# Block-sparse attention with an MLP behind it: diagonal mask by affine_select, built-in gelu, casting loads, and the second MLP product next to the next batch's attention

## The chip, the cores and the metric

One core of one Trainium2 chip. The metric is device time in microseconds (us) of one execution. Most numbers inside an execution come from one profiled execution of each kernel, which is called "the trace". Times below are medians of 4 executions for a changed kernel and of 4 to 7 for the kernel before, on the same chip. With one core an execution is called slow when it is over 1.5% above the fastest one of the same kernel.

## The reference

Four batches, eight heads, 768 tokens, head size 64. Per head, keys are averaged over blocks of 64 tokens; each query keeps its own block and the three blocks with the best gate score, and of those only what is causal. The result (3072 tokens of 512 features) goes through a two-layer MLP with the tanh form of gelu.

```python
k_rep = k.reshape(B, H, n_blocks, block, D).mean(axis=3)
gate_scores = np.einsum('bhsd,bhnd->bhsn', q, k_rep)
... # blocks after the query's own: -1e9; top 3 and the own block are kept
scores = scale * np.matmul(q, k.transpose(0, 1, 3, 2))
mask = mask & (pos[:, None] >= pos[None, :])
... # softmax over what is kept, times v, heads put side by side: x
h = x @ w_in                                   # 512 -> 2048
g = 0.5 * h * (1.0 + np.tanh(c * (h + 0.044715 * h * h * h)))
return g @ w_out                               # 2048 -> 512
```

## The kernel before

It works on pairs of heads, 16 pairs in all, four to a batch. For each pair it transposes q and k on TensorE, makes the block sums of k and the gate scores in fp32, turns the choice of blocks into 12 extra rows of q and k (so that one matmul gives scores with the block mask), adds the causal triangle by one more matmul for each diagonal block, applies Exp, and multiplies by v (this product is called PV below). A column of ones in v gives the softmax's denominator.

The MLP of a finished batch is cut into 30 pieces per batch (S1, the first product with gelu; S2, the second product), and one piece is emitted between the stages of the next batch's attention. In batch 0 there are no pieces yet, and matmuls on zeros that nothing reads stand in.

```python
def emit_moe(n):
    for _ in range(n):
        if moe_q:
            moe_q.pop(0)()
        elif warm[0] > 0:                      # batch 0: fillers
            ...
                nc.tensor.matmul(wt[:, 0:128], ident16, zsrc, start=True, stop=True)
...
# weights: fp32 loads, then one cast each on ScalarE
nc.sync.dma_start(out=win32, in_=moe_w_in.rearrange("(ci p) f -> p ci f", p=128))
nc.sync.dma_start(out=wout32, in_=moe_w_out.rearrange("(fi p) c -> p fi c", p=128))
nc.scalar.copy(out=w_in16, in_=win32)
nc.scalar.copy(out=w_out16, in_=wout32)
...
# block sums of k: fp32 matmuls against a two-column indicator
for c in range(NC):
    nc.tensor.matmul(mt[:, 456 + 2 * c:458 + 2 * c],
                     k_sd[:, c].rearrange("p h d -> p (h d)"), blockind,
                     start=True, stop=True)
...
# scores of one group of two key chunks, then the triangle, then Exp
    nc.tensor.matmul(st[:, cb:cb + 128], ident16, tri16, start=False, stop=True)
nc.scalar.activation(out=at[:, 0:wa + wb], in_=st[:, 0:wa + wb],
                     func=AF.Exp, bias=0.0, scale=SCALE)
...
# S1: 256 tokens x 256 features at a time; gelu in four operations
nc.scalar.square(out=hsq, in_=hflat)
nc.vector.scalar_tensor_tensor(out=uu, in0=hsq, scalar=CC, in1=hflat, op0=ALU.add, op1=ALU.mult)
nc.scalar.activation(out=th, in_=uu, func=AF.Tanh, bias=0.0, scale=C2)
nc.vector.scalar_tensor_tensor(out=..., in0=th, scalar=1.0, in1=hflat, op0=ALU.add, op1=ALU.mult)
```

The softmax here doesn't subtract the row's maximum and nothing guards it: scores larger than these inputs give would overflow.

## Time and profile before

| | |
|---|---|
| time | 401.99 us median of 3 before the prediction (398.93 to 406.75); 404.37 us of 4 with the run beside the changed kernel |
| TensorE busy | 372.6 us, 93% of the span |
| weight casts on ScalarE | 2 x 7.02 us |
| composed gelu, per 512 columns | 596 + 681 + 629 + about 684 ns |
| clock granted to TensorE | mean 0.95; half from 61.5 to 102.5 us but for two windows |

The page's first two parts, before: busy us with the share of the span, then two rows of 40 slices of the span, in which a digit is the busy share in tenths (9 is 90% or more), and PEclk is the granted TensorE clock in tenths.

```profile
PE 372.6 (93%) x3344; PEld 274.3 (68%) x3344; DVE 248.8 (62%) x676; ACT 265.2 (66%) x395; POOL 6.3 (2%) x30
...
PE   5999986899989999999898999999988999999996
...
PEclk9999996555999999999999989999999999999999
```

And the chain of work that ended last, by engine:

```profile
PE 69%; ACT 14%; DVE 12%; issue 2%; DMA 1%; SPq 0%; ACTq 0%
```

TensorE is at work almost all the time; of the recorded clock only slices 6 to 9, some 60 to 100 us, are low. (The profile holds the clock from its first record on, at 20.5 us in before; the 9s ahead of it are no measurement. There the fp32 transposes of q and k follow each other at 213 ns, and later, at full clock, at 109 ns: TensorE ran at half clock until then, and the mean clocks quoted are too high by that.) The windows view of before gives the busy time of each engine in a stretch (start:end, length, then each engine's busy us with its number of instructions, the granted clock, the DMA share, GB/s):

```profile
core 0: us, PE busy (x) PEld busy (x) DVE busy (x) ACT busy (x) POOL busy (x), PEclk, DMA share, GB/s
102.50:152.70 50.20, 47.37 (x452) 34.28 (x449) 36.49 (x94) 36.71 (x58) 0.00 (x0) 1.00 0.30 66
152.70:234.20 81.50, 77.33 (x736) 55.86 (x736) 52.68 (x157) 55.42 (x87) 0.00 (x0) 1.00 0.23 59
234.20:310.00 75.80, 72.68 (x697) 53.55 (x697) 53.45 (x154) 53.40 (x84) 0.00 (x0) 0.98 0.04 15
310.00:402.00 92.00, 85.77 (x611) 54.28 (x609) 57.17 (x95) 59.69 (x108) 0.00 (x0) 1.00 0.10 35
```

In each stretch TensorE is 93 to 96% busy at or near full clock, so after the first hundred microseconds it is TensorE's work that sets the time. What went wrong before that shows in the ScalarE timeline of before (start, length, engine, line, operation, out<-in, then in brackets the idle time ahead of it and what ended it):

```profile
54.32 7.02 ACT L167 CAST w_in_138<-win_180 128x8192 f16<-128x8192 f32 x1
61.23 0.93 ACT L292 ACTIVATE at_1_2_963<-st_1_2_962 128x896 f16<-128x896 f32 x1
...
63.92 7.02 ACT L168 CAST w_out_139<-wout_181 128x8192 f16<-128x8192 f32 x1
...
73.41 0.92 ACT L292 ACTIVATE at_0_0_1114<-st_0_0_1113 128x896 f16<-128x896 f32 x1
```

Two casts of 7 us stand among the Exps. The last Exp of a pair (61.23) waits behind the first cast, the first Exp of the next pair (73.41) behind the second, and the next pair therefore comes 24.2 us after the one before in place of 12.3.

### The profile page before, as it was taken

The numbers are of one execution on the slowest core, as the hardware profiler recorded it, in microseconds if no ns is written. First come the engines' busy times: TensorE is split into PE (matmuls) and PEld (weight loads), VectorE is DVE, ScalarE is ACT, GpSimd is POOL, SyncE is SP. The second block draws the span as 40 slices with busy tenths as digits, with TensorE's granted clock in tenths as the row PEclk, the third lists the DMA queues.
The fourth block names the chain that finished last, engine by engine and source line by source line (L and its number), as shares of the span: only waits on it lengthen the run. The fifth ranks groups of instructions, "written<-read, shape, count | busy, mean of one in ns | idle before, by whom it ended". The sixth has DMA issues, their size and how long they took to land.

```text
span 401.9 us, 8201 instructions
## 1 busy us (share of the span) xinstructions
PE 372.6 (93%) x3344; PEld 274.3 (68%) x3344; DVE 248.8 (62%) x676; ACT 265.2 (66%) x395; POOL 6.3 (2%) x30
## 2 busy tenths in 40 slices
PE   5999986899989999999898999999988999999996
PEld 4988865587855876675776677667576675675672
DVE  2556633346672894686688279568657546955963
ACT  2166698636674893884787579388568755865782
POOL 6000000000000000000000000000000000000000
PEclk9999996555999999999999989999999999999999
DMA  9999999923003914052400100000000010011011
GB/s 184 219 323 392 305 203 211 182 46 76 0 2 108 181 41 106 27 119 68 104 2 2 54 1 2 28 28 0 29 29 0 2 54 26 28 52 55 0 55 52
DMA packets 81350, 34.08 MB, mean 85 GB/s; under 512 B 75681, under 2 KB 75681, under 8 KB 80801
## 3 DMA queue, kind: packets, MB, share of 16 engines
q1 hardware_dynamic: 81312, 33.56, 34.5%
q8 instruction: 26, 0.43, 0.5%
q14 instruction: 12, 0.09, 0.1%
HBM read 27.26 MB, written 6.29 MB: 83 GB/s over the span
## 4 chain that ended last, share of the span: by engine, by line
PE 69%; ACT 14%; DVE 12%; issue 2%; DMA 1%; SPq 0%; ACTq 0%
PE hps L340 12%; DVE uu L350 4%; ACT hsq L348 3%; ACT w_in_138 L167 2%; ACT th L355 1%; DMA k_sd_65<-in_k_dram 1%; PE ops_0_4091 L367 1%; PE ops_0_2666 L367 1%; PE ops_0_5090 L367 1%; PE ops_0_4922 L367 1%; PE ops_0_5426 L367 1%; PE ops_0_5258 L367 1%; PE ops_0_4754 L367 1%; PE ops_0_4563 L367 1%; PE ops_0_1702 L367 1%
## 5 line engine op out<-in xcount | busy, mean ns | idle before, releaser
L350 DVE SCALAR_TENSOR_TENSOR uu<-hsq,hps 128x512 f16<-128x512 f16 x96 | 65.4, 681 | 51.8 <-ACT hsq L348 50.6
L340 PEld LDWEIGHTS <-w_in_138 128*128 128x128 f16 x768 | 71.9, 100 | 22.0 <-ACT w_in_138 L167 3.1
L355 ACT ACTIVATE th<-uu 128x512 f16<-128x512 f16 x96 | 60.2, 629 | 14.2 <-DVE uu L350 14.2
L348 ACT ACTIVATE hsq<-hps 128x512 f16<-128x512 f32 x96 | 56.7, 596 | 18.0 <-PE hps L340 17.7
L340 PE MATMUL hps<-xT_134,w_in_138 128*128 128x256 f16 x192 | 53.6, 279 | 6.9 <-ACT w_in_138 L167 2.9
L340 PE MATMUL hps<-xT_136,w_in_138 128*128 128x256 f16 x192 | 53.4, 279 | 0.6 <-DVE xT_136 L324 0.6
L340 PE MATMUL hps<-xT_135,w_in_138 128*128 128x256 f16 x192 | 53.6, 279 | 0.0
L340 PE MATMUL hps<-xT_137,w_in_138 128*128 128x256 f16 x192 | 53.4, 278 | 0.0
L288 PEld LDWEIGHTS <-ident_105 128*128 128x128 f16 x192 | 20.0, 104 | 10.1 <-issue 4.2
L315 DVE TENSOR_TENSOR xns<-xnr,zrec 128x384 f16<-128x384 f16 x32 | 17.7, 554 | 4.4 <-ACT xnr L313 4.3
L321 PEld LDWEIGHTS <-xns 128*64 128x64 f16 x192 | 12.0, 113 | 10.8 <-DVE xns L315 9.8
L152 PEld LDWEIGHTS <-ident_105 128*128 128x128 f16 x208 | 15.2, 112 | 0.5
L282 PEld LDWEIGHTS <-kT_0_1_145 76*128 76x128 f16 x64 | 6.7, 113 | 2.8 <-issue 1.4
L282 PEld LDWEIGHTS <-kT_0_0_144 76*128 76x128 f16 x64 | 6.6, 111 | 2.1 <-issue 0.9
L282 PEld LDWEIGHTS <-kT_1_1_147 76*128 76x128 f16 x64 | 6.1, 103 | 1.9 <-issue 0.3
L356 DVE SCALAR_TENSOR_TENSOR gT_3581<-th,hps 128x512 f16<-128x512 f16 x8 | 5.5, 684 | 2.5 <-ACT th L355 2.5
L168 ACT CAST w_out_139<-wout_181 128x8192 f16<-128x8192 f32 x1 | 7.0, 7022 | 0.0
L167 ACT CAST w_in_138<-win_180 128x8192 f16<-128x8192 f32 x1 | 7.0, 7021 | 0.0
L356 DVE SCALAR_TENSOR_TENSOR gT_1272<-th,hps 128x512 f16<-128x512 f16 x8 | 5.4, 684 | 2.6 <-ACT th L355 2.5
L282 PEld LDWEIGHTS <-kT_1_0_146 76*128 76x128 f16 x64 | 5.8, 100 | 1.6
L356 DVE SCALAR_TENSOR_TENSOR gT_2431<-th,hps 128x512 f16<-128x512 f16 x8 | 5.5, 683 | 1.4 <-ACT th L355 1.3
L180 PE MATMUL wq_218<-ident_100,q_sd_64 128*128 128x128 f32 x6 | 1.5, 426 | 4.7 <-DMA q_sd_64<-in_q_dram 4.7
(1156 smaller groups left out, 929.1 us busy)
## 6 DMA issues: line engine op xcount, KB each, us to landing
out_dram<-osb SPq DMA_DIRECT2D x24, 256.0 KB, 2.0
win_180<-in_moe_w_in_dram SPq DMA_DIRECT2D x1, 4096.0 KB, 13.9
wout_181<-in_moe_w_out_dram SPq DMA_DIRECT2D x1, 4096.0 KB, 24.2
q_sd_64<-in_q_dram SPq DMA_DIRECT2D x2, 192.0 KB, 3.0
k_sd_65<-in_k_dram SPq DMA_DIRECT2D x2, 192.0 KB, 3.7
v_sd_66<-in_v_dram SPq DMA_DIRECT2D x2, 192.0 KB, 4.2
q_sd_73<-in_q_dram SPq DMA_DIRECT2D x2, 192.0 KB, 4.5
k_sd_74<-in_k_dram SPq DMA_DIRECT2D x2, 192.0 KB, 4.6
```

The source lines that it names most:

```text
L152: nc.tensor.matmul(wt[:, 0:128], ident16, zsrc, start=True, stop=True)
L167: nc.scalar.copy(out=w_in16, in_=win32)
L282: nc.tensor.matmul(st[:, u0:u1], kt[0:76, s0:s0 + 128], qt[0:76, s0 + (u0 - cb):s0 + (u1 - cb)], start=True, stop=(bank != tri_bank),)
L288: nc.tensor.matmul(st[:, cb:cb + 128], ident16, tri16, start=False, stop=True,)
L315: nc.vector.tensor_tensor(out=xns, in0=xnr, in1=zrec.unsqueeze(2).to_broadcast([128, NC, 64]), op=ALU.mult,)
L321: nc.tensor.transpose(pvq16[0:64, qc * 128:(qc + 1) * 128], xns[:, qc, :], ident16)
L340: nc.tensor.matmul(hps[:, j, :], w_in16[:, ci, (fi + j) * 128:(fi + j + 1) * 128], xT[ci][:, t0:t0 + TCH], start=(ci == 0), stop=(ci == 3),)
L348: nc.scalar.square(out=hsq, in_=hflat)
L350: nc.vector.scalar_tensor_tensor(out=uu, in0=hsq, scalar=CC, in1=hflat, op0=ALU.add, op1=ALU.mult,)
L355: nc.scalar.activation(out=th, in_=uu, func=AF.Tanh, bias=0.0, scale=C2)
L356: nc.vector.scalar_tensor_tensor(out=gT[:, fi:fi + 2, :].rearrange("p a w -> p (a w)"), in0=th, scalar=1.0, in1=hflat, op0=ALU.add, op1=AL ...
L367: nc.tensor.matmul(ops, gT[:, fi, ti * 128:(ti + 1) * 128], w_out16[:, fi, :], start=(fi == 0), stop=(fi == NF - 1),)
```

## The change

The intent is to take work off TensorE and off the composed gelu, and to arrange the MLP anew. Diff, cut to its core:

```diff
-    nc.sync.dma_start(out=win32, ...); nc.scalar.copy(out=w_in16, in_=win32)   # and w_out
+    def load_w_in():
+        nc.gpsimd.dma_start(
+            out=w_in16, in_=moe_w_in.rearrange("(ci p) f -> p ci f", p=128))   # casts on the way
+    def load_v(p):                        # v too: fp32 in memory, fp16 in SBUF
+            nc.gpsimd.dma_start(out=v16[p % NB][:, :, hh, 0:64], in_=v[b, 2 * hp + hh]...)
...
-            nc.tensor.matmul(mt[:, 456 + 2 * c:458 + 2 * c], k_sd[:, c]..., blockind, ...)
+        nc.vector.tensor_reduce(
+            out=ks, in_=wk[:, 0:S].rearrange("p (n w) -> p n w", w=64),
+            op=ALU.add, axis=AXL.X)
...
-                nc.tensor.matmul(st[:, cb:cb + 128], ident16, tri16, start=False, stop=True)
                 ex = nc.scalar.activation(out=at[:, 0:wa + wb], ..., func=AF.Exp, ...)
+                for cb in (0, wa):
+                    nc.gpsimd.affine_select(
+                        out=at[:, cb:cb + 128], in_=at[:, cb:cb + 128],
+                        compare_op=ALU.is_ge, fill=0.0,
+                        base=0, pattern=[[1, 128]], channel_multiplier=-1)
+                # PV of one head accumulates in one PSUM bank, group by group, right after its Exp
...
-        # square, scalar_tensor_tensor, tanh, scalar_tensor_tensor; 0.5 at the end
+            g = nc.scalar.activation(out=gT[b][:, f, :], in_=hps[:, 0:S],
+                                     func=AF.Gelu_apprx_tanh, bias=0.0, scale=1.0)
...
+    for b in range(B):
+        for hp in range(HP):
+            p = b * HP + hp
+            load(p + 4)
+            if p == 2:
+                load_w_out()
+            pre(p + 2)                    # transposes, gate, mask of the pair after next
+            heads(p)
+        if b > 0:
+            s2(b - 1)                     # fills gaps of this batch's attention
+        s1(b)                             # all 16 blocks in a row: one table switch
+    s2(B - 1)
```

Normalisation now handles both heads of a pair at once (six output transposes in place of twelve), the gate is not computed for the first 128 queries (they keep all their causal blocks anyway), and the fillers of batch 0 are gone. The scheduler that lays out the instructions puts S2's matmuls, which stand behind the pairs in the program text of a batch, into gaps that it foresees in attention.

## The prediction

> **What bounds the kernel now.** TensorE, in three stages. The page gives it 93% busy, and 69% of the chain that ended last. Windows view: from 153 to 234 us four head pairs and their share of the MoE pass, 81.5 us, TensorE busy 77.3, clock 1.00; from 310 to 402 us only MoE is left, 14.4 us per 256 tokens (chain of waits: 326.1, 340.5, 354.9). Between: ScalarE's two weight casts, 7.02 us each, from 54 to 68 us stop TensorE, its clock falls to 0.5 and stays there most of the time until 102 us (0.62 and 0.59 in the windows 60:80 and 80:100).
>
> **Removed from TensorE**, by spacings in the timeline at full clock: block sums by matmul 1.29 us per pair (to a VectorE reduction), triangle matmuls 12 x 57 ns = 0.7, half the output transposes 0.36. A pair falls from about 8.5 to 6.0 us, some 40 us over 16 pairs, and 208 filler matmuls (12 us) go. Both MoE products keep their work: 1.33 us per 128 rows of d_ff and batch, 21.3 per batch; second product 16 x 222 ns = 3.6 per 128 tokens, 21.3 per batch.
> **Removed elsewhere:** per 512 columns Square 596, Tanh 629 and two VectorE operations of 681 ns become one Gelu of about 0.85 us per 768 (estimate from Exp, 0.92 for 896). The casts go.
> **Added:** 12 affine_selects per pair on GpSimd, 0.30 us each (setup ones in the trace), between Exp and PV; GpSimd-issued cast DMAs for v and the weights (the Trainium skill, "DMA: Bandwidth & Descriptors", SWDGE vs HWDGE vs iDMA: casting DMAs are GpSimd's alone; no run shows their issue time yet, I guess 1 to 3 us per v DMA); seven table loads more, 1.28 us.
>
> **Critical path after.** S1 (21.3 us per batch) and the last S2 (21.3 + 3) stay TensorE-bound. Attention becomes bound by a chain, not by an engine: two PSUM tiles serve q, k and scores alike. Instruction order shows per pair: six Exps with scores held behind PV, which waits for the selects, 5.6 us; then select, PV of head 0, issue of a v DMA (which waits for that PV and stands before head 1's select), select, PV of head 1, reciprocal, k copy (0.95), normalisation, transposes, next scores: 7 to 8 us. So about 13.4 us per pair, against 11.3 us of TensorE with S2. The first selects also queue behind eight v DMAs and both weight DMAs: first pair done at 38, not 30.
> Sum: 38 + three pairs at a partly half clock, 16 each, + 8 + S1 22 = 116; batches 1 and 2: 3 + 53 + 22 = 78 each; batch 3 (last pairs have no preparation): 73; tail 24. About 367; I take a little off for unmodelled overlap.
>
> **Predicted: 363 us, 80% range 333 to 397.** Faster by over 2%: 0.87; within 2%: 0.08; slower: 0.05.
>
> **Signs.** TensorE busy share falls to 75-85%, ScalarE to about 45%; VectorE about 50%; GpSimd waits name PE. S1 stretches of about 21 us with TensorE over 95% busy, four of them. Clock at 0.5 in much of the first attention (before 90 us), mostly 1.0 afterwards: the Trainium skill, "TensorE: Matmul & The Clock Gate", Part 1, has windows of 3.4 us; the before windows agree with that[...]. Waits of TensorE name affine_select and VectorE's k copy or normalisation. No 7 us casts.
>
> **What would make it wrong.** A v DMA issue of 4 us or more on GpSimd: above 395. Under 1 us: near 340. Clock at half in batches 1 to 3 too: attention there 22 us per pair, over 420. A better interleaving of S2 into the chain's gaps: 335. Weight DMAs slow to land (v of pair 4 shares their semaphores): start-up plus 10 to 20.

## The result, and the profile after

The changed kernel takes 357.81 us (median of 4, 357.56 to 358.47), the kernel before 404.37 us on the same chip (median of 4, 398.93 to 408.13; by the rule of 1.5% two of these four, 406.75 and 408.13, count as slow). Ratio 0.897, 95% interval 0.889 to 0.905. Ratios in this document are the mean time of one kernel's fast runs over that of the other's of the same rounds, so not quite the ratio of the medians that are quoted.

The page after, same parts, with the DMA row (mean busy share of the core's 16 DMA engines):

```profile
PE 319.0 (90%) x2352; PEld 195.1 (55%) x2352; DVE 154.6 (43%) x456; ACT 159.8 (45%) x184; POOL 88.0 (25%) x252
...
PE   3625977988999999999999999989999999999995
...
PEclk9999967667999999999999999999999999999999
DMA  9999999583004548823004832341000000100012
...
PE 72%; ACT 9%; issue 6%; DMA 5%; POOL 3%; DVE 3%; SPq 2%; ACTq 0%; POOLq 0%
```

TensorE is busy 53.6 us less (372.6 to 319.0), the span is 46.0 us shorter (401.9 to 355.9). The windows view of after: attention of batch 0, its S1 with the way to the next pair, then batch 1 from its first Exp to the table load ahead of S1, and from there to the first Exp of batch 2.

```profile
34.24:84.10 49.86, 44.60 (x339) 31.67 (x338) 28.19 (x97) 23.89 (x28) 17.74 (x52) 0.73 0.98 145
84.10:114.15 30.05, 28.63 (x183) 17.17 (x181) 7.15 (x23) 16.17 (x19) 2.23 (x4) 0.99 0.23 34
114.15:156.10 41.95, 39.34 (x377) 24.50 (x376) 28.77 (x85) 23.45 (x27) 17.67 (x52) 1.00 0.60 97
156.10:191.40 35.30, 34.62 (x217) 20.14 (x215) 8.76 (x26) 16.33 (x21) 2.23 (x4) 1.00 0.23 44
```

The first line has half clocks (0.73; about 0.64, an estimate, if the unrecorded 9.5 us up to 43.7 us are counted as half) and a DMA share of 0.98; from batch 1 on the clock is full and TensorE 94 and 98% busy. To see where the time came from, take three stretches, with the traces' times:

| stretch | before | after | difference |
|---|---|---|---|
| start to the first Exp | 22.7 | 34.2 | +11.5 |
| from there to the first Exp of pair 4, without S1 of batch 0 (20.1 us, from its first Gelu at 88.4 to 108.5 us, only in after) | 69.3 | 59.8 | -9.5 |
| the rest (12 pairs, all of the MLP; S1 of batch 0 added to after) | 309.9 | 261.8 | -48.1 |
| in the last row, TensorE busy (windows view) | 293.6 | 249.8 | -43.8 |

So almost all of the gain is TensorE work that is no longer there: 43.8 of the 48.1 us. And 11.5 us are lost at the start, which I had put down to something else. The TensorE timeline of after shows that wait:

```profile
25.46 1.30 PE L171 MATMUL wq_327<-ident_103,q_sd_242 128*128 128x128 f32 x5 [6.68 <-DMA q_sd_242<-in_q_dram]
```

TensorE stands for 6.68 us until the q of pair 2 has landed. The transposes of pair 2 stand in its order ahead of the scores of pair 0. SyncE's timeline shows when that q was issued (8.24 us, in two issues), and that the next two issues took 11.34 us; below it, the list of DMA issues of after (KB each, median us from issue to landing) shows what was under way:

```profile
8.24 1.72 SPq L68 DMA_DIRECT2D q_sd_242<-in_q_dram  x2
10.00 11.34 SPq L68 DMA_DIRECT2D k_sd_246<-in_k_dram  x2
```

```profile
w_in_181<-in_moe_w_in_dram POOLq DMA_DIRECT2D x1, 2048.0 KB, 15.7
w_out_182<-in_moe_w_out_dram POOLq DMA_DIRECT2D x1, 2048.0 KB, 33.7
...
q_sd_94<-in_q_dram SPq DMA_DIRECT2D x2, 192.0 KB, 3.7
...
q_sd_242<-in_q_dram SPq DMA_DIRECT2D x2, 192.0 KB, 11.1
```

The first q load lands after 3.7 us, that of pair 2 after 11.1 us as the median of its two issues; the later of the two landed at 25.3 us, 16.2 us after its issue. The weights now come at the same time, while the DMA row is at 9. The Trainium skill, "DMA: Bandwidth & Descriptors", section "Issuing engines are not separate DMA queues", says that loads issued by different engines run on the same 16 DMA engines and interleave. This trace agrees: SyncE's loads slow down though GpSimd issued the big ones.

Inside attention one order stands out, here at the end of a pair in batch 1 of after (a timeline of all engines, cut):

```profile
143.36 0.92 ACT L242 ACTIVATE at_1_2_1613<-st_1_2_1612 128x896 f16<-128x896 f32 x1
...
144.51 0.84 POOL L78 DMA_DIRECT2D v_161<-in_v_dram  x1 [0.62 <-PE pv_0_1536 L258]
...
145.36 0.55 POOL L252 TENSOR_SCALAR_AFFINE_SELECT at_1_2_1613<-at_1_2_1613 128x128 f16<-128x128 f16 x2
145.72 0.52 PE L258 MATMUL pv_1_1537<-v_161,at_1_2_1613 128*128 128x65 f16 x7 [0.60 <-POOL at_1_2_1613 L252]
```

The last Exp ends at 144.28, but its selects begin at 145.36, because GpSimd first waits for a PV and then issues a load of v for a later pair, 0.84 us. TensorE idles 0.60 us for it.

### The profile page after: what moved, and what is told of

It is laid out like the page before. It is cut to its first block, busy times and chain, and to the rows that moved or that the text cites. A ratio compares the mean times of both kernels' runs of the same rounds, so it can differ in the third digit from the quotient of the medians.

```text
span 355.9 us, 5980 instructions
## 1 busy us (share of the span) xinstructions
PE 319.0 (90%) x2352; PEld 195.1 (55%) x2352; DVE 154.6 (43%) x456; ACT 159.8 (45%) x184; POOL 88.0 (25%) x252
## 4 chain that ended last, share of the span: by engine, by line
PE 72%; ACT 9%; issue 6%; DMA 5%; POOL 3%; DVE 3%; SPq 2%; ACTq 0%; POOLq 0%
DMA q_sd_242<-in_q_dram 5%; SPq L68 2%; PE ops_5_2858 L302 1%; PE ops_5_1908 L302 1%; PE ops_5_3953 L302 1%; PE ops_4_3933 L302 1%; PE ops_1_3873 L302 1%; PE ops_4_3652 L302 1%; PE ops_3_3913 L302 1%; PE ops_2_3893 L302 1%; PE ops_0_3853 L302 1%; PE ops_5_3672 L302 1%; PE ops_3_3632 L302 1%; PE ops_3_2818 L302 1%; PE ops_3_1868 L302 1%
## 5 line engine op out<-in xcount | busy, mean ns | idle before, releaser
L288 PEld LDWEIGHTS <-w_in_181 128*128 128x128 f16 x512 | 50.1, 98 | 35.0 <-issue 2.0
L302 PEld LDWEIGHTS <-gT_3692 128*128 128x128 f16 x96 | 9.4, 98 | 11.2
L302 PEld LDWEIGHTS <-gT_2878 128*128 128x128 f16 x96 | 9.3, 98 | 7.8
L302 PEld LDWEIGHTS <-gT_978 128*128 128x128 f16 x96 | 9.3, 99 | 7.4 <-issue 0.2
L302 PEld LDWEIGHTS <-gT_1928 128*128 128x128 f16 x96 | 9.3, 99 | 7.4 <-issue 0.2
L160 DVE TENSOR_REDUCE ks_1152<-wk_1145 128x12 f32<-128x768 f32 x1 | 1.0, 958 | 20.5 <-PE wk_1145 L156 20.5
L160 DVE TENSOR_REDUCE ks_3046<-wk_3039 128x12 f32<-128x768 f32 x1 | 1.0, 958 | 19.9 <-PE wk_3039 L156 19.9
L160 DVE TENSOR_REDUCE ks_2102<-wk_2095 128x12 f32<-128x768 f32 x1 | 1.0, 956 | 19.9 <-PE wk_2095 L156 19.9
L252 POOL TENSOR_SCALAR_AFFINE_SELECT at_0_0_2155<-at_0_0_2155 128x128 f16<-128x128 f16 x2 | 0.5, 282 | 33.0 <-ACT at_0_0_2155 L242 33.0
L252 POOL TENSOR_SCALAR_AFFINE_SELECT at_0_0_3099<-at_0_0_3099 128x128 f16<-128x128 f16 x2 | 0.5, 282 | 33.0 <-ACT at_0_0_3099 L242 33.0
L78 POOL DMA_DIRECT2D v_137<-in_v_dram x8 | 6.8, 856 | 4.3 <-PE wq_1326 L171 1.0
L78 POOL DMA_DIRECT2D v_173<-in_v_dram x8 | 6.7, 843 | 4.9 <-PE pv_0_873 L258 1.4
L78 POOL DMA_DIRECT2D v_149<-in_v_dram x8 | 6.8, 855 | 4.3 <-PE pv_0_538 L258 1.2
L78 POOL DMA_DIRECT2D v_161<-in_v_dram x8 | 6.7, 838 | 4.5 <-PE pv_0_706 L258 1.4
L171 PE MATMUL wq_327<-ident_103,q_sd_242 128*128 128x128 f32 x6 | 1.8, 431 | 6.7 <-DMA q_sd_242<-in_q_dram 6.7
L252 POOL TENSOR_SCALAR_AFFINE_SELECT at_0_0_1205<-at_0_0_1205 128x128 f16<-128x128 f16 x2 | 0.5, 282 | 28.2 <-ACT at_0_0_1205 L242 28.2
L168 ACT CAST kT_1_160<-wk_314 64x768 f16<-64x768 f32 x1 | 0.8, 795 | 14.5 <-DVE kT_0_159 L167 14.5
L242 ACT ACT_TABLE_LOAD x3 | 3.8, 1283 | 5.5 <-PE st_0_0_1204 L237 1.8
L156 PE MATMUL wk_183<-ident_103,k_sd_91 128*128 128x128 f32 x6 | 1.5, 425 | 4.6 <-POOL madd_138 L135 4.6
L168 ACT ACT_TABLE_LOAD x1 | 1.3, 1283 | 9.5 <-DVE ksb_192 L164 9.5
L252 POOL TENSOR_SCALAR_AFFINE_SELECT at_0_0_374<-at_0_0_374 128x128 f16<-128x128 f16 x2 | 0.5, 287 | 19.4 <-ACT at_0_0_374 L242 19.4
```

What stands on the lines that cost most here:

```text
L78: nc.gpsimd.dma_start(out=v16[p % NB][:, :, hh, 0:64], in_=v[b, 2 * hp + hh].rearrange("(c p) d -> p c d", p=128),)
L156: nc.tensor.transpose(wk[:, c * 128:(c + 1) * 128], k_sd[:, c].rearrange("p h d -> p (h d)"), ident32)
L160: nc.vector.tensor_reduce(out=ks, in_=wk[:, 0:S].rearrange("p (n w) -> p n w", w=64), op=ALU.add, axis=AXL.X)
L168: nc.scalar.copy(out=kT16[i][1][0:64, :], in_=wk[64:128, 0:S])
L171: nc.tensor.transpose(wq[:, c * 128:(c + 1) * 128], q_sd[:, c].rearrange("p h d -> p (h d)"), ident32)
L242: ex = nc.scalar.activation(out=at[:, 0:wa + wb], in_=st[:, 0:wa + wb], func=AF.Exp, bias=0.0, scale=SCALE)
```

## The experiments

Twelve kernels were run, all with correct results, each timed in three rounds against the kernel before on the same chip. The table gives the first Exp of pairs 0, 4, 8, 12 and 15 and the end, in us of each trace; it is used throughout. The period of a batch is the distance from pair 4 to pair 8. The runs were made in three calls (e1, e2, e3), each on another chip, and within each the kernel before was run again (medians 403.82, 405.34, 406.02), so between calls the ratios are the safer comparison. Where a change acts only on a part, the traces are: from the first Exp of pair 4 to the end after, e1_control, e1_wlate and e2_fill, which are alike there, take 241.7, 241.8, 241.8 and 242.0 us. The start is not so steady: in the six kernels that load the weights as after does, the first Exp comes at 28.8 to 34.7 us.

| run | median us | ratio to before (95%) | pair 0 | 4 | 8 | 12 | 15 | end |
|---|---|---|---|---|---|---|---|---|
| before | 404.37 | 1 | 22.7 | 92.0 | 174.2 | 260.7 | 311.4 | 401.9 |
| after | 357.81 | 0.897 (0.889-0.905) | 34.2 | 114.2 | 191.4 | 269.0 | 293.1 | 355.9 |
| e1_control | 356.46 | 0.878 (0.869-0.887) | 32.2 | 112.5 | 189.8 | 267.5 | 291.6 | 354.4 |
| e1_wlate | 348.51 | 0.863 (0.858-0.868) | 26.9 | 104.5 | 181.7 | 259.4 | 283.5 | 346.3 |
| e1_tri | 354.68 | 0.880 (0.872-0.887) | 28.8 | 107.5 | 185.1 | 265.4 | 290.5 | 353.3 |
| e1_bcast | 401.33 | 0.993 (0.987-0.999) | 41.7 | 93.3 | 171.3 | 258.1 | 308.7 | 399.1 |
| e2_bcastl | 387.29 | 0.949 (0.936-0.962) | 21.3 | 75.6 | 152.2 | 238.8 | 289.4 | 379.8 |
| e2_tanh | 467.75 | 1.154 (1.143-1.164) | 29.3 | 141.7 | 250.7 | 360.1 | 386.0 | 461.7 |
| e2_seq | 397.83 | 0.975 (0.963-0.986) | 34.7 | 117.9 | 211.7 | 305.7 | 343.6 | 397.1 |
| e2_fill | 347.04 | 0.857 (0.852-0.862) | 24.8 | 103.7 | 181.0 | 258.9 | 282.9 | 345.7 |
| e3_va | 338.88 | 0.834 (0.827-0.841) | 24.9 | 102.8 | 177.0 | 251.2 | 275.2 | 338.0 |
| e3_ksum | 368.03 | 0.902 (0.892-0.911) | 31.4 | 112.4 | 192.3 | 272.6 | 298.4 | 362.1 |
| e3_bgelu | 396.99 | 0.974 (0.964-0.984) | 23.0 | 92.3 | 172.5 | 253.3 | 305.9 | 393.1 |
| e3_best | 335.46 | 0.823 (0.816-0.831) | 24.6 | 99.2 | 173.4 | 247.8 | 271.8 | 334.6 |

(The kernel after showed 0.897 in its first comparison and 0.878 as the control. The ratios of the quoted medians are 0.885 and 0.883; the first comparison had few fast executions of before, and the control's own executions differ by 2%.)

### e1_control: the kernel after, again (no edit)

> The kernel after, unchanged, as the yardstick on this chip. Every theory expects 357 to 359 us and a ratio to the kernel before of 0.89 to 0.905.

Measured: 356.46 us (351.59 to 359.01), ratio 0.878; a little under the expected range. It is the yardstick for the three runs beside it.

### e1_wlate: hold the weight loads back

```diff
     def load_w_in():
+        nc.gpsimd.tensor_copy(out=w_in16[0:1, 0, 0:1],          # waits for pair 3's q
+                              in_=P[3]["q"][0:1, 0, 0, 0:1])
         nc.gpsimd.dma_start(out=w_in16, ...)
...
     def load_w_out():
-        nc.gpsimd.dma_start(out=w_out16, ...)
+        dw = nc.gpsimd.dma_start(out=w_out16, ...)              # and: after the selects of pair 0
...
     load(2)
-    load_w_in()
     load(3)
     pre(1)
+    load_w_in()
```

> The kernel after, with the w_in casting load held until the q of pair 3 has landed and the w_out load issued after the selects of pair 0. Theory (the weight loads share the DMA engines with the first q and k loads, pair 2's q lands at 25.3 us, and its transposes stand ahead of pair 0's scores on TensorE): the first Exp comes at 22 to 26 us in place of 34.2, TensorE no longer waits for q_sd of pair 2, and the time falls by 7 to 11 us, to 347 to 351 us. Rival (what I predicted: the first Exps and selects wait for the GpSimd queue and for VectorE's preparation): first Exp stays within 2 us of 34.2 and the time within 2 us of the control.

Measured: 348.51 us, 8 us under the control; the first Exp came at 26.9 us, 5.3 us earlier than the control's. TensorE's waits in the first 30 us of this run (engine and line, what it waited for: us in total, times, longest):

```profile
PE wk L163 <- DMA k_sd<-in_k_dram: 4.9, 1, 4.9
PE st L245 <- ACT kT L175: 3.5, 1, 3.5
...
PE wq L178 <- DMA q_sd<-in_q_dram: 0.3, 1, 0.3
```

The wait for pair 2's q fell from 6.7 us in after, and 5.1 in the control, to 0.3 us, and w_out, issued later, landed after 20.0 us in place of 34.7 (control). In the four variants of the kernel after that hold the weights back the whole q of pair 2 has landed at 15.4 to 16.4 us, in the six that don't at 19.7 to 25.8 us. So the shared DMA engines were the cause of the late start, and my "first selects queue behind the loads on GpSimd" was not: in after, GpSimd had done all its issues at 15.9 us and then waited 19.4 us for the first Exp. The Exp itself came 1 us later than the theory's range; what is left is the wait for ScalarE's copy of k, 3.5 us, and that copy is again one of pair 2, which stands ahead of pair 0's scores. Putting pair 2's preparation behind them would be the next thing to try; it was not run.

### e1_tri: the triangle matmul back in place of the selects

```diff
+                    nc.tensor.matmul(st[:, cb:cb + 128], ident16, tri16,
+                                     start=False, stop=True)
...
-                for cb in (0, wa):
-                    nc.gpsimd.affine_select(out=at[:, cb:cb + 128], ...)
```

> The kernel after, with the selects on GpSimd taken out and the triangle matmul of before put back (12 accumulating 128x128 matmuls a pair, some 0.7 us of TensorE). Theory A (attention is bound by the chain Exp, select, PV; TensorE has gaps there): losing the selects takes 0.55 us plus a hand-over out of the chain, the added matmuls fall into gaps: the time is equal or up to 10 us shorter (348 to 359 us). Rival B (TensorE work is what counts, the selects are free): 16 pairs times 0.7 = 11 us more, 367 to 371 us.

Measured: 354.68 us, ratio 0.880 against the control's 0.878: the same. The pieces are not the same. The first three pairs of batch 1 take 10.3, 11.1 and 12.0 us in place of the control's 11.4, 11.7 and 12.3, so the selects do lengthen the chain. But from the last pair's first Exp to the next batch it takes 44.2 us in place of 41.8, and the period of the batch is 77.6 against 77.3 us. The faster pairs take in fewer S2 matmuls, and those run at the end of the batch. The equal total hides something, though. From the first Exp of pair 4 to the end this run takes 245.8 us against the control's 241.8: 0.3 us more in batch 1, 2.7 in batch 2 (with 6.8 us at half clock from 218.5 us on), 1.0 in the rest. It makes this up at the start, where its first Exp comes 3.4 us before the control's, because TensorE waits less for pair 2's q. The longest wait is the last number, first of the control, then of this run:

```profile
PE wq L171 <- DMA q_sd<-in_q_dram: 5.4, 2, 5.1
PE wq L176 <- DMA q_sd<-in_q_dram: 1.8, 2, 1.5
```

The edit doesn't touch that load, and it lands at different times in kernels with the same start, so this is not counted as the edit's doing. The change from matmul to select was thus worth some 4 us in these two traces, and the total shows nothing of it.

### e1_bcast and e2_bcastl: the casts alone, in the kernel before

```diff
-        nc.sync.dma_start(out=win32, ...)          # and wout32
-        nc.scalar.copy(out=w_in16, in_=win32)      # and w_out16
+    nc.gpsimd.tensor_copy(out=w_in16[0:1, 0, 0:1], in_=P[3]["q_sd"][0:1, 0, 0, 0:1])  # e2_bcastl only
+    nc.gpsimd.dma_start(out=w_in16, ...)
+    nc.gpsimd.tensor_copy(out=w_out16[0:1, 0, 0:1], in_=w_in16[0:1, 0, 0:1])          # e2_bcastl only
+    nc.gpsimd.dma_start(out=w_out16, ...)
```

> The kernel before, with only the weights loaded by casting DMAs in place of the two fp32 loads and two 7.02 us casts on ScalarE. Theory (the two casts hold ScalarE for 14 us at 54 to 68 us, TensorE stops behind it and then runs at half clock until 102 us): the time falls by 14 to 30 us, to 374 to 390 us, and the cold stretch from 61 to 102 us is shorter. Rival (the cold stretch comes from the attention chain itself and the casts only fill ScalarE's idle time): within 5 us of before.

Measured: 401.33 us, ratio 0.993: as the rival said, and yet the rival is wrong. The first Exp moved from 22.7 to 41.7 us, and the first Exp of pair 4 hardly moved (92.0 to 93.3): between the two, 17.7 us were gained, and at the start 19.0 us were lost to the same contention as in after. In before the weight loads had stood behind all q, k and v loads of the first four pairs in one queue; moved to GpSimd, they run beside them. Hence the second run.

> The kernel before with casting weight loads once more, but now held until the q of pair 3 has landed, so that they do not share the DMA engines with the first loads. In e1_bcast the time from the first Exp of pair 0 to that of pair 4 fell from 69.3 to 51.6 us, while the first Exp moved from 22.7 to 41.7 us. Theory (the casts cost some 18 us, and the early loads gave it all back at the start): first Exp at 22 to 24 us, first Exp of pair 4 at 74 to 77, and the time falls to 380 to 389 us. Rival (the gain of e1_bcast after the first Exp came only from the work that had been prepared during the long start): first Exp of pair 4 at 85 us or later and a time above 394 us.

Measured: 387.29 us (381.52 to 389.19; two of the four executions count as slow, being 1.5% above the fastest), ratio 0.949. First Exp at 21.3, first Exp of pair 4 at 75.6 us: 54.3 us in place of 69.3. The clock row of its page, where before has "6555" in slices 6 to 9:

```profile
PEclk9699999989999999999999899999999999999999
```

The casts, with the cold clock behind them, cost 15 us in before up to pair 4, and some 5.5 us more from there to pair 8 (82.2 to 76.6 us). The kernel became 18 us (medians) to some 20 us (means of the fast executions) faster than before; this theory stands, and the rival falls. How much is the casts' own time and how much the cold clock, this run does not separate.

### e2_tanh and e3_bgelu: the gelu, undone and alone

```diff
 # e2_tanh: the kernel after
-            g = nc.scalar.activation(..., func=AF.Gelu_apprx_tanh, ...)
+            nc.scalar.square(out=hsq, in_=hps[:, 0:S])
+            nc.vector.scalar_tensor_tensor(out=uu, in0=hsq, scalar=1.0 / A_CUBE, in1=hps[:, 0:S], ...)
+            g = nc.scalar.activation(out=th, in_=uu, func=AF.Tanh, ...)
+            nc.vector.scalar_tensor_tensor(out=gT[b][:, f, :], in0=th, scalar=1.0, in1=hps[:, 0:S], ...)
...
-            nc.vector.tensor_copy(out=osb, in_=ops)
+            nc.vector.tensor_scalar(out=osb, in0=ops, scalar1=0.5, ...)
 # e3_bgelu: the kernel before
-        nc.scalar.square(out=hsq, in_=hflat)               # and uu, th, gT
+        nc.scalar.activation(out=gT[:, fi:fi + 2, :]..., in_=hflat, func=AF.Gelu_apprx_tanh, ...)
...
-        nc.scalar.mul(out=osb, in_=ops, mul=0.5)
+        nc.scalar.copy(out=osb, in_=ops)
```

> The kernel after with the composed gelu (square, two VectorE operations, tanh) put back in place of the one Gelu. Theory (the built-in gelu is what lets S1 run at TensorE's pace of 1.30 us per 128x768 block, since the composed one needs some 1.7 to 1.8 us of ScalarE and 1.9 to 2 us of VectorE a block and holds a PSUM tile through all four steps, of which there are only two): S1 goes from 21 us to 31 to 45 us in each batch, less 9 us of table loads in all: 393 to 440 us. Rival (gelu is off the critical path, since TensorE was 93% busy before as well): within 10 us of the control, 348 to 368 us.

Measured: 467.75 us, 111 us above the control and above the 440 that I had put at the top. From the last pair of a batch to the next batch it took 72.3 us in place of 41.8. Its timeline, in S1 of batch 1, cut to one round:

```profile
194.26 0.81 ACT L296 ACTIVATE hsq<-hps 128x768 f16<-128x768 f32 x1 [9.31 <-PE hps L291]
195.11 0.95 DVE L298 SCALAR_TENSOR_TENSOR uu<-hsq,hps 128x768 f16<-128x768 f16 x1 [0.58 <-ACT hsq L296]
195.56 0.81 ACT L296 ACTIVATE hsq<-hps 128x768 f16<-128x768 f32 x1 [0.49 <-PE hps L291]
196.27 0.83 ACT L302 ACTIVATE th<-uu 128x768 f16<-128x768 f16 x1
196.41 0.95 DVE L298 SCALAR_TENSOR_TENSOR uu<-hsq,hps 128x768 f16<-128x768 f16 x1 [0.35 <-ACT hsq L296]
197.28 1.94 DVE L304 SCALAR_TENSOR_TENSOR gT<-th,hps 128x768 f16<-128x768 f16 x2
...
198.28 2.77 PE L291 MATMUL hps<-xT,w_in 128*128 128x512 f16 x16 [2.76 <-DVE gT L304]
```

Square, multiply, tanh, multiply: the last of the four reads the PSUM tile once more, so that the tile comes free only then. With two tiles, both go through the four steps, TensorE waits 2.76 us, fills both (2.77), and all begins again: 5.6 us for two blocks where the built-in gelu lets TensorE go on at 1.30 us a block. The clock suffers too: in four of the seven rounds from 198 to 246 us the 16 matmuls run in part at half clock, 4.4 us in place of 2.77, and the round takes 7.3 us. I had added up engine time; what counts here is the length of the chain over the number of tiles. Before escaped this, since it spread its gelus over attention and had five tiles in its tail.

> The kernel before with the built-in Gelu alone in place of the composed one; the order of work stays, so ScalarE goes to and fro between Exp and Gelu and the build has 46 table loads in place of 1 (1.28 us each, 59 us of ScalarE), against 59 us of ScalarE and 131 us of VectorE saved. Theory (the built-in gelu pays only together with the new order, in which all 16 Gelus of a batch follow each other): not faster than before, 400 to 425 us. Rival (the composed gelu's VectorE and ScalarE work was itself what held before back): 375 to 395 us.

Measured: 396.99 us, ratio 0.974: between the two, so neither theory holds as stated. ScalarE's groups in this run (line, engine, operation, count, then busy us, mean ns):

```profile
L347 ACT ACTIVATE gT<-hps 128x512 f16<-128x512 f32 x96 | 56.6, 601 | 12.9 <-PE hps L340 12.4
L347 ACT ACT_TABLE_LOAD x23 | 29.5, 1283 | 0.7 <-PE hps L340 0.3
L292 ACT ACT_TABLE_LOAD x22 | 28.2, 1283 | 0.3
```

ScalarE gives back as table loads (59 us) what it saves on square and tanh, and is busier than before (275.1 against 265.2 us). VectorE loses nearly half of its work (248.8 to 134.2 us). That, it seems, is what bought the 2.6%. The Trainium skill, "ScalarE: Activation LUTs", section "Table sets: the hidden batching unit", advises to batch activations by set; its Exp and tanh share a set: before has one table load for all its Exps and tanhs, this run 46, the kernel after, with 16 Gelus in a row, 8.

### e2_seq: S2 not next to attention

```diff
-        if b > 0:
-            s2(b - 1)
         s1(b)
-    s2(B - 1)
+        s2(b)
```

> The kernel after with S2 of a batch issued straight after S1 of the same batch, not next to the next batch's attention; all other work is the same. Theory (in attention TensorE waits for the chain of scores, Exp, select, PV and for the pair boundary, and the S2 matmuls fill those waits and keep the clock up): the attention pairs of batches 1 and 2 take as long as before without S2, 8 to 10 us warm or up to 13.5 us cold, so that each batch with S2's 21 us added becomes 10 to 18 us longer: 375 to 405 us. Rival (the same TensorE work in another order costs the same): within 5 us of the control.

Measured: 397.83 us; the fast executions 392.78 and 396.83, ratio 0.975. That is some 40 us above the control's fast executions, of which a good 16 us in each of batches 1 and 2. The windows view of this run (a slow execution, so only its inner shape is used): the first pair of batch 1, into which the scheduler now puts nearly all of S2, the second, the third, and the rest of the batch.

```profile
117.90:141.30 23.40, 20.66 (x152) 11.34 (x151) 10.31 (x30) 6.12 (x9) 4.99 (x14) 1.00 0.36 93
141.30:154.30 13.00, 11.28 (x92) 7.96 (x91) 8.74 (x28) 6.23 (x8) 5.09 (x14) 0.69 0.57 81
154.30:168.60 14.30, 12.35 (x92) 9.02 (x91) 8.30 (x27) 6.16 (x8) 4.98 (x14) 0.62 0.62 80
168.60:211.70 43.10, 41.88 (x258) 25.10 (x257) 10.15 (x30) 21.62 (x26) 4.98 (x14) 0.86 0.19 29
```

The second and third pair, with no S2 in them, take 13.0 and 14.3 us at a clock of 0.69 and 0.62: longer than the 11.7 and 12.3 us of the control's, which contain S2 work. S2 next to attention thus costs these pairs no time; how much of that is the filling of gaps and how much the clock that it keeps up, this run does not separate. TensorE counts as 87 and 86% busy in these two windows, and still the clock was halved.

### e2_fill: fillers in batch 0

```diff
 # e1_wlate, and:
+        else:                                   # b == 0, where s2(b - 1) would stand
+            for ti in range(8):
+                fl = opsp.tile([128, 512], FP32, tag="ops", name=f"fill_{ti}")
+                for f in range(16):
+                    nc.tensor.matmul(fl, ident16, zsrc, start=(f == 0), stop=(f == 15))
```

> The kernel of e1_wlate with 128 matmuls of 512 columns on zeros that nothing reads, placed by the scheduler into batch 0's gaps just as the S2 matmuls are in batches 1 and 2. Theory (batch 0's pairs take 13.5 to 14 us in place of 11.4 to 12.3 because TensorE idles, falls to half clock and then streams at half speed): the clock is full from some 10 us on, pairs 0 to 3 take 11 to 12.5 us each, and the time falls by 5 to 10 us, to 339 to 344 us. Rival (batch 0's pairs are slow because of the chain through ScalarE, GpSimd and VectorE, whatever the clock): pairs stay at 13.5 to 14 us and the time is equal to or above that of e1_wlate, 347 us and more.

Measured: 347.04 us, 1.5 us under e1_wlate's 348.51: closer to the rival. The clock did what the theory said:

```profile
PEclk9999999999999999999999999999999999999999
```

But the pairs of batch 0 took 13.9, 12.0 and 12.3 us (e1_wlate: 14.1, 13.8, 11.9), and from the last pair to the next batch 40.7 us in place of 37.8. In the trace 29 of the 128 fillers start after the first Exp of the last pair, 16 of them after S1's first matmul, where TensorE has enough to do; at full clock 29 times 216 ns (the spacing of S2's matmuls in after) is 6.3 us (an estimate), which would eat up most of what the full clock gains.

### e3_va: the v loads behind the selects

```diff
-            nc.gpsimd.dma_start(out=v16[p % NB][:, :, hh, 0:64], ...)
+            dv = nc.gpsimd.dma_start(out=v16[p % NB][:, :, hh, 0:64], ...)
+            if p >= 4:                           # in GpSimd's order after pair p-4's last select
+                tc.add_manual_dep(dv.ins, last_sel[p - 4], ...)
```

> The kernel of e1_wlate with one order fixed: the two casting v loads that GpSimd issues for a later pair come after the last select of the running pair, not one of them (0.84 us) ahead of it. Theory (in the pairs of batches 1 and 2 the chain Exp, select, PV, reciprocal, transposes, next scores ends last, and that load issue stands in it): pairs become 0.4 to 0.85 us shorter (11.0 us in place of 11.4 to 12.3) and the time falls by 5 to 10 us, to 338 to 344 us. Rival (TensorE's own work in attention plus S2 is the limit there, and a shorter chain only moves S2 matmuls to the end of the batch, as the triangle run hinted): pairs may be shorter, the stretch from the last pair's first Exp to the next batch is longer by the same, batch period stays at 77 us, time within 2 us of 348.5.

(This run holds the edit of e1_wlate too.) Measured: 338.88 us, 9.6 us under e1_wlate (8.3 in the traces); ratio 0.834 against 0.863. The pairs of batch 1 take 10.5, 11.0 and 11.6 us, the end of the batch 41.0 us in place of 41.8: this time both got shorter, and the period went from 77.3 to 74.2 us. The same two windows as above, batch 1 of e3_va:

```profile
102.80:142.50 39.70, 38.92 (x377) 24.55 (x376) 28.61 (x85) 23.46 (x28) 17.50 (x52) 1.00 0.63 102
142.50:177.00 34.50, 34.47 (x217) 20.12 (x214) 8.76 (x26) 16.33 (x20) 2.16 (x4) 1.00 0.24 45
```

TensorE is now busy 98 and 99.9% of the time; its idle time per batch went from 3.3 us (77.25 less 73.96 in after) to 0.8. Of the 8.3 us between the traces, 6.6 lie after the first Exp of pair 4 (241.8 to 235.2 us); the rest is an earlier first Exp, which this edit can't have made, since it moves only loads that come later. Here the rival, which said that TensorE's work was the limit, was wrong for the last 3 us of each batch: the wait that the v load caused was TensorE idle time, which no S2 matmul had filled.

### e3_ksum: the block sums back on TensorE

```diff
-        nc.vector.tensor_reduce(out=ks, in_=wk[:, 0:S].rearrange("p (n w) -> p n w", w=64), ...)
+        for c in range(NC):
+            nc.tensor.matmul(wk[:, S + 2 * c:S + 2 * c + 2],
+                             k_sd[:, c].rearrange("p h d -> p (h d)"), blockind,
+                             start=True, stop=True)
```

> The kernel after with the block sums of k back on TensorE, six fp32 matmuls a pair against a two-column indicator as in before (1.29 us a pair at full clock), and the 0.95 us VectorE reduction gone. Theory (TensorE's work is what the time is made of, and moving the block sums off it paid): up to 16 times 1.29 = 21 us longer, at least half of it: 366 to 378 us, and the batch period goes from 77.3 to about 82 us. Rival (as with the triangle, TensorE has room in attention and the reduction costs the chain as much): within 4 us of the control, 352 to 361 us.

Measured: 368.03 us, ratio 0.902 against the control's 0.878, some 2.7% or 9.5 us; the two traces differ by 7.7 us. The first comparison of after had the ratio 0.897, so the ratio alone would not settle it; the traces do, since from the first Exp of pair 4 to the end this run takes 249.7 us against 241.7 to 242.0. The period of a batch is 79.9 us in place of 77.3, that is +2.6, half of four times 1.29. The windows of batch 1:

```profile
112.40:152.60 40.20, 38.65 (x396) 26.69 (x394) 25.39 (x83) 23.47 (x28) 18.00 (x53) 1.00 0.57 88
152.60:192.30 39.70, 39.27 (x243) 23.16 (x242) 8.46 (x25) 16.31 (x20) 1.88 (x4) 1.00 0.24 52
```

Against the windows of after, TensorE is busy 3.96 us longer per batch (38.65 + 39.27 against 39.34 + 34.62), and its idle time fell from 3.3 to 2.0 us, presumably since the VectorE reduction (0.95 us) is out of the chain at the pair's boundary (the first three pairs take 10.7, 11.2 and 11.3 us). So of the 3.96 us that come off TensorE per batch, 2.6 reach the time, and the rest is paid back by a longer chain. Moving the block sums was worth 8 to 10 us.

### e3_best: the parts that helped, together

```diff
 # e1_wlate and e3_va (e3_va already holds both), and of e2_fill:
-            for ti in range(8):
+            for ti in range(6):                 # 96 fillers
```

> The parts that helped, together: weights held back (e1_wlate), v loads behind the selects (e3_va), and 96 in place of 128 filler matmuls, so that none stands in the last pair of batch 0 or in S1, where e2_fill lost 2 to 3 us. Theory: e2_fill's clock (0.998) with pairs of 11 to 12.5 us in batch 0 and 38 us from pair 3 to pair 4: 3 to 4 us below e3_va and e2_fill, 335 to 343 us. Rival (the chain bounds batch 0, whatever the clock): no less than e3_va or e2_fill, whichever is lower.

This is e1_wlate, e3_va and 96 fillers, none of which lies in the last pair of batch 0 or in S1. Measured: 335.46 us (333.69 to 336.29), ratio 0.823; 3.4 us below e3_va. The pairs of batch 0 take 13.9, 11.6 and 11.3 us, and 37.9 us from the last to the next batch. TensorE is busy 320.9 of 334.6 us. This version beats both kernels: 0.823 against after's 0.897 or 0.878 in ratios to before. Why pair 0 takes 13.9 us whatever the clock stays open.

## Why the prediction was right or wrong

**The time and the direction were right.** 363 us (333 to 397) was predicted, 357.8 measured, faster by 10%. The predicted stages, against the trace of after (they add up to 369, not to the 367 of the prediction):

| term of the sum | predicted | measured |
|---|---|---|
| first pair done | 38 | 48.9 |
| three pairs more, to S1 | 48 | 39.5 |
| S1 and the way to the first Exp of batch 1 | 30 | 25.8 |
| sum so far | 116 | 114.2 |
| batches 1, 2 | 78 each | 77.2, 77.6 |
| batch 3, up to the end of S1 | 73 | 63.3 |
| tail | 24 | 23.6 |

**TensorE bounds the kernel, and removed TensorE work is what pays: right.** In the steady part 43.8 of 48.1 us are TensorE busy time. Twelve pairs at the predicted 2.5 us are 30 of them, and the half clock that before still had from 92.2 to 102.5 us makes another 5 (an estimate: half of that stretch). By what each matmul writes, with the time up to the next matmul's start, the attention's matmuls account for some 34 us of the difference and S1's for some 10, these 5 of half clock among them. By undoing parts: the block sums were worth 8 to 10 us (e3_ksum), where 16 times 1.29 = 21 us had been counted; the triangle was worth nothing in the total and some 4 us from pair 4 on (e1_tri), where 11 us over all pairs, 8 of them from pair 4 on, had been counted, because the select that replaced it lengthened the chain. The halved output transposes and the shorter gate were not tested.

**"ScalarE's two weight casts ... stop TensorE, its clock falls to 0.5": right,** 18 to 20 us (e2_bcastl). The change did not get all of that at once, since its casting loads were issued at the start (e1_bcast).

**"The first selects also queue behind eight v DMAs and both weight DMAs: first pair done at 38": this step failed.** The issues were done at 15.9 us (0.84 us per v load, 0.77 and 1.2 us for the weights; my guess had been 1 to 3 us per v load). The first Exp waited for data: the weight loads share the DMA engines with q and k, pair 2's q landed at 25.3 us, and pair 2's transposes stand ahead of pair 0's scores. The prediction had slow weight loads only among its risks, and there for another reason ("v of pair 4 shares their semaphores"). e1_wlate won 8 us of it back.

**"Three pairs at a partly half clock, 16 each": the term was too large.** They took 13.6, 12.4 and 13.5 us. The clock was indeed half in much of batch 0, but full clock there saves only 3 to 4 us in all (e3_best against e3_va).

These errors had opposite signs (+10.9 for the first pair, -8.5 for the others, -4.2 for S1 and what follows), and the sum for batch 0 came out right by luck.

**"Attention becomes bound by a chain", 13.4 us per pair against 11.3 of TensorE: half right.** The pairs of batches 1 and 2 take 11.4 to 12.3 us, and TensorE is 94% busy in them. The chain is real: TensorE's idle time there came from it, and 3.1 and 3.5 us in batches 1 and 2 were won by moving the v loads in it (e3_va). But the periods of 78 us were met because S2 work that did not fit into the shorter pairs ran at the end of the batch: a pair that is faster by chain alone hands its S2 matmuls on (e1_tri). Three pairs of batch 1 took 35.4 us where 13.4 each, 40, had been counted, and the rest of the batch 41.8 where 38 had: here too errors of opposite sign met. The sign "busy share falls to 75-85%" was wrong accordingly: 90%.

**S2 beside attention's chain: right, and worth more than I said.** Undoing it costs some 40 us (e2_seq).

**The built-in gelu: its 0.85 us per 768 columns (measured 0.81) and S1 at TensorE's pace were right** (20.1 us per batch, TensorE 97% busy). Its worth depends on the order: alone in before 2.6% (e3_bgelu), taken out of after 31% longer (e2_tanh, 467.75 to 356.46 us).

**Batch 3, 73 us: too large.** The last two pairs, which prepare no later pair, took 6.9 and 6.5 us. This term alone is 9.7 us, more than the whole difference between 363 and 357.8.

## What to carry to other kernels

Where one engine is nearly full, ask of each operation taken off it what replaces it in the chain: here at least half of what the triangle's removal should have given was paid back, and a third of the block sums'. Moving a large load to another issuing engine takes away its place behind the urgent loads; it has to be held back on purpose, and the rest of a change cannot be judged before that is done. And when a time comes out as predicted, compare the terms of the sum: here errors of about 10 us cancelled, and the one at the start was the easiest 8 us to win.

## What the Trainium skill lacked or had wrong

- "TensorE: Matmul & The Clock Gate", Part 1, gives windows of 3413 ns and says that the clock is halved after one or more idle windows. The traces agree on the grid (all stretches of a clock but the last, which the end cuts off, are multiples of 3.41 us, in after for example 43.73 to 47.15) and on the two values, 1.0 and 0.5. But "idle" is not what the profile's busy share shows: in e2_seq the clock was 0.69 and 0.62 on average in pairs in which TensorE counts as 87 and 86% busy. The page says that frequent short idle gaps can make the clock go to and fro, but has no figure for how much work a window needs.
- "DMA: Bandwidth & Descriptors", section "SWDGE vs HWDGE vs iDMA", states that casting DMAs must be issued from GpSimd, as this kernel does. The page calls the making of descriptors small and variable and gives about 1 us to the first byte on this path, but has no figure by size or pattern for how long GpSimd's own queue is held by such an issue: 0.84 us for 96 KB of v in 6 x 64-element rows, 0.77 and 1.2 us for the two weights of 2048 KB. Where GpSimd does other work in a chain, as here, moving the v loads was worth 6.6 us from pair 4 on (e3_va against e1_wlate).
- No page that I found has a duration for affine_select on GpSimd: 0.28 to 0.32 us for 128x128 fp16 but for a few longer ones, median 0.29.
- "ScalarE: Activation LUTs", sections "What ACT_TABLE_LOAD costs" and "Table sets: the hidden batching unit": 1283 ns per load and 186 ns + 0.833 ns per column agree with the traces (1283 ns; Gelu of 768 columns 811 ns against 826, Exp of 896 columns 916 ns against 932). The first section adds a drain of about 1380 ns to every switch of sets; in e3_bgelu all but one of 45 loads start within 19 ns of the end of the operation before and the next operation starts 11 or 12 ns after them, so a switch takes some 1.3 us. The list of sets says only that the tanh form of gelu is apart from gelu's own set, not which set holds it; here it does not share one with Exp, since 46 loads went to and fro in e3_bgelu.
